# Eight experts on one core: weights as stationary 64-column blocks, and five of eight weight transfers behind a small transfer

## The chip, the cores and the metric

The kernel runs on one core of a Trainium2 chip. The metric is the device time of one execution in microseconds (us); less is better. Engines: PE (TensorE matmul), PEld (its weight load), DVE (VectorE), ACT (ScalarE), POOL (GpSimd), SP (SyncE, which issues transfers).

## What is computed

A recurrence (RWKV-7) over 768 steps for 4 x 8 heads gives 3072 rows x of 320 numbers. Each row goes to the one of eight experts with the largest gate; of an expert's rows the 80 with the largest gate weight are kept. Cut to what matters here, the rest is

```python
for e in range(E):                       # 8 experts
    tok_idx = ...                        # at most 80 rows
    h = np.maximum(x[tok_idx] @ w1[e], 0.0)                # 320 -> 1024
    out[tok_idx] = gate_w[tok_idx, None] * (h @ w2[e])     # 1024 -> 320
```

All numbers are float32; rows that are not kept stay zero in `out`.

## The kernel before

The kernel has three stages. In the first the recurrence is worked out in 24 units of 64 steps. Its instructions are recorded in a `Plan`, which puts them in an order by estimated times, and are then issued in that order. It ends with the ranking of gate weights (`rank_early` to `rank_last`, on DVE): `extract` (L842) takes the ten groups of eight largest values out of a row with MAX8 and MATCH_REPLACE8. The last two extracts work on `pair_a` and `pair_b` (L824), which are two buffers of `raww` in the pool `hold`. Gate and x rows of the last units go to DRAM (`x_rows`, L817).

Then the pool `hold` is closed, and a pool `wpool` takes its memory: all eight experts' weights get tiles of their own and are loaded by SP in turn (`load_expert`, L974 to L982; per expert `w1` as 128 x 2 x 1024, the remaining 64 rows of `w1` in two halves `w1r` on partitions 0 to 63 and 64 to 127, and `w2` as 128 x 8 x 320). Beside that, the second stage turns the ranking into lists of rows `idx_g` and `idx_s` (L1010 to L1051).

The third stage is the experts (from L1054 on). POOL gathers the 80 rows of each expert (`gather`). For expert e, `turn_x` turns the rows, `first_layer` holds x stationary (128 x 80) and moves the weights in 512 columns, ACT applies the ReLU, `turn_h` turns h in eight transposes with two DVE copies, `second_layer` holds h stationary and moves `w2` in 320 columns, DVE scales the result by the gate weight and POOL scatters it to `out`. The order in this stage is that of a scheduler, which starts from the order of the code:

```python
for e in range(E + 1):
    if e < E:
        first_layer(e)
    if e + 1 < E:
        turn_x(e + 1)
    if e > 0:
        second_layer(e - 1)
    if e < E:
        turn_h(e)
```

Of the kernel before, what the change touches and what calls it, by code (L numbers as in the profile page):

```python
# [145 lines left out]
def kernel(  # L146
# [77 lines left out]
    with ExitStack() as p1:  # L224
# [28 lines left out]
        def at(name, n):  # L253
            name, n = key_of(name, n)
            return buf[name][n % RINGS[name]]
# [7 lines left out]
        def bank(key):  # L263
            return plan.home[key]
# [556 lines left out]
            add(*args, sooner=LISTS[len(ranked)], **kw)  # L821

        ranked = []
        pair_a, pair_b = at("raww", NM), at("raww", NM + 1)  # L824

        def clear_tail(z):
            addr("POOL", 0.4, 0.1, z, lambda: nc.gpsimd.memset(la[:, capr:], 0.0), (), [("la", 0)])
# [1 line left out]
        def turn_gates(pieces, dst, key, z, bis):  # L829
            kc = ("gp", pieces[0][0])  # L830
            rows = pieces[0][1] * E

            def go():
                for j, (m0, nu) in enumerate(pieces):
                    nc.tensor.transpose(ps[0:rows, bank(kc), 128 * j : 128 * j + 128],
                                        gates[:, m0 : m0 + nu, :].rearrange("p m e -> p (m e)"), ident)
            addr("PE", 0.2 * len(pieces), 0.2, z, go, [("gates", b_) for b_ in bis], (), (kc, 1))
            addr("DVE", 0.25 + 0.001 * 128 * len(pieces), 0.1, z,
                lambda: nc.vector.tensor_copy(dst, ps[0:rows, bank(kc), 0 : 128 * len(pieces)]), [kc], [key])

        def extract(dst, src, z, src_key, dst_key):
            cols = src.shape[-1]  # L842
# [52 lines left out]
        def rank_late():  # L895
            ranked.append(1)
            z = 22 * PER
            turn_gates([(20, 1), (21, 1)], pair_a[0:E, 0:256], ("raww", NM), z, [5])
            clear_tail(z)
            extract(la[0:E], pair_a[0:E, 0:256], z, ("raww", NM), LA)  # L900
            merge(8, tops[0], tops[0], z, A0, A0)

        def rank_last():
            ranked.append(1)
            z = 24 * PER
            turn_gates([(22, 1), (23, 1)], pair_b[0:E, 0:256], ("raww", NM + 1), z, [6])
            extract(tops[1], pair_b[0:E, 0:256], z, ("raww", NM + 1), ("tops", 1))

        def late_adds():
            def late_consts():  # L910
# [70 lines left out]
        nc.sync.dma_start(w2, moe_w2[e].rearrange("(c p) d -> p c d", p=128))  # L981
        weights[e] = w1, w1r, w2  # L982

    for e in range(E):
        load_expert(e)

    idx_g = const.tile([cap, E], I32, name="idx_g")
# [71 lines left out]
    rows, xes, hs, hts = {}, {}, {}, {}  # L1059

    def gather(e):
        rows[e] = fs.tile([cap, XW], F32, name="rows", tag="rows", bufs=8)
        nc.gpsimd.indirect_dma_start(
            out=rows[e][:, 0:XW], out_offset=None, in_=x_dram[:, :],
            in_offset=bass.IndirectOffsetOnAxis(ap=idx_g[:, e : e + 1], axis=0))

    def turn_x(e):
# [8 lines left out]
        xes[e] = fs.tile([128, 3, cap], F32, name="xe", tag="xe")  # L1076
        nc.vector.tensor_copy(xes[e], xp)  # L1077

    def first_layer(e):
# [6 lines left out]
        for j in range(2):  # L1086
            half = slice(64 * j, 64 * j + 64)
            nc.tensor.matmul(hp[j], lhsT=xe[half, 2, :], rhs=w1r[half, :], start=False, stop=True)  # L1088
        hs[e] = fs.tile([cap, F], F32, name="h", tag="h")
        for j in range(2):  # L1090
            nc.scalar.activation(hs[e][:, FH * j : FH * j + FH], hp[j], Act.Relu)  # L1091

    def turn_h(e):
        h = hs.pop(e)
        hts[e] = fs.tile([128, FK, cap], F32, name="hT", tag="hT")
        for j in range(2):
            tp = ps_t.tile([128, FK // 2, cap], F32, name="tp", tag=f"t{j}")
            for f in range(FK // 2):
                o = FH * j + 128 * f
                nc.tensor.transpose(tp[:, f, :], h[:, o : o + 128], ident[:cap, :cap])  # L1100
            nc.vector.tensor_copy(hts[e][:, FK // 2 * j : FK // 2 * (j + 1), :], tp)  # L1101

    def second_layer(e):
        w2 = weights[e][2]
        hT = hts.pop(e)
        yp = ps_y.tile([cap, DM], F32, name="yp", tag="y")
        for f in range(FK):
            nc.tensor.matmul(yp, lhsT=hT[:, f, :], rhs=w2[:, f, :], start=f == 0, stop=f == FK - 1)  # L1108
        y = fs.tile([cap, DM], F32, name="y", tag="y")
        nc.vector.tensor_scalar_mul(y, yp, rows[e][:, DM : DM + 1])  # L1110
        nc.gpsimd.indirect_dma_start(  # L1111
            out=out[:, :], out_offset=bass.IndirectOffsetOnAxis(ap=idx_s[:, e : e + 1], axis=0),
            in_=y[:, :], element_offset=0, bounds_check=N - 1, oob_is_err=False, in_offset=None)

    for e in range(E):
        gather(e)
    turn_x(0)
    for e in range(E + 1):
        if e < E:
            first_layer(e)  # L1120
        if e + 1 < E:
            turn_x(e + 1)
        if e > 0:
            second_layer(e - 1)
        if e < E:
            turn_h(e)


# [24 lines left out]
```

## Time and profile before

| | |
|---|---|
| median of 3 runs (lowest, highest) | 560.91 us (559.71, 563.14) |
| the profiled execution, its own time | 561.64 us |
| its span | 559.6 us |
| PE busy | 425.6 us, 76% of the span |
| PEld busy | 331.6 us, 59% |
| DVE busy | 312.5 us, 56% |
| POOL busy | 224.1 us, 40% |
| ACT busy | 186.0 us, 33% |
| read and written in DRAM | 53.26 MB and 18.13 MB |

The span is what the profiler recorded of one execution; the time of that execution is 2.0 us longer. The shares are means over three stages with different limits, so a change to one stage is to be read from that stage's own rows. Times in the rows are us from the start of the span.

### The profile page before, as it was taken

To read this page: it belongs to the slowest core of one execution; us is meant where nothing else is said; L and a number is where in the kernel's file an instruction comes from. 1 tells how busy PE (TensorE), PEld (TensorE's weight loads), DVE (VectorE), ACT (ScalarE), POOL (GpSimd) and SP (SyncE) were. 2 spreads that over 40 slices of the span, in tenths; PEclk is the share of its full clock that TensorE was granted. 3 is DMA by queue.
4 is the path that set the end of the run, shared out by engine and by line. 5 is a ranking of instruction groups with operands and counts; after the bars stand their busy time and mean duration, and the time that the engine had idled before them with its cause. 6 is when DMAs were issued, how large, how long until landed. Compare 5 with 4: busy or idle time off the path is not lost. (4 is left out here: it accounts for less than half of the span.)

```text
span 559.6 us, 22079 instructions
## 1 busy us (share of the span) xinstructions
PE 425.6 (76%) x9617; PEld 331.6 (59%) x9617; DVE 312.5 (56%) x706; ACT 186.0 (33%) x361; POOL 224.1 (40%) x393
## 2 busy tenths in 40 slices
PE   2644089797928988889799998998895003999996
PEld 2543078686717877778687887887784002344443
DVE  4867977444703855684476644966678981121211
ACT  2432064353512453444443643445231000101010
POOL 7010011788388410898699516981000005010101
PEclk9978569798976999999899999999699555899999
DMA  8775367556593477676577374327200049999300
GB/s 133 113 116 112 64 154 133 99 94 133 96 243 81 99 174 134 149 132 117 133 143 172 100 132 116 75 44 161 71 16 27 23 143 342 326 332 344 104 15 16
DMA packets 241444, 72.91 MB, mean 130 GB/s; under 512 B 217908, under 2 KB 235716, under 8 KB 241348
## 3 DMA queue, kind: packets, MB, share of 16 engines
q1 hardware_dynamic: 211428, 65.50, 51.6%
q10 hardware_dynamic: 29152, 4.36, 4.9%
q0 software_dynamic: 768, 1.64, 1.0%
q8 instruction: 76, 1.25, 0.9%
q14 instruction: 20, 0.16, 0.1%
HBM read 53.26 MB, written 18.13 MB: 128 GB/s over the span
## 5 line engine op out<-in xcount | busy, mean ns | idle before, releaser
L498 POOL TENSOR_TENSOR tmp<-lt 128x30 f32<-128x30 f32 (+9 forms) x150 | 84.0, 560 | 61.0 <-DMA lt<-blocks 50.3
L500 POOL TENSOR_TENSOR lt<-lt,tmp 128x30 f32<-128x30 f32 (+9 forms) x150 | 88.8, 592 | 11.8
L707 DVE TENSOR_TENSOR UL<-ps,mask 128x832 f32<-128x832 f32 x24 | 24.5, 1022 | 54.0 <-PE ps L702 54.0
L758 PE MATMUL ps<-wsel,xT 128*128 128x192 f32 x192 | 40.7, 360 | 2.3 <-DVE xT L748 1.4
L1111 POOL DMA_INDIRECT out_dram<-y,idx_s x8 | 7.3, 917 | 74.6 <-DVE y L1110 74.6
L758 PEld LDWEIGHTS ps<-wsel,xT 128*128 128x128 f32 x192 | 34.2, 208 | 4.3 <-DVE xT L748 1.7
L369 DVE TENSOR_TENSOR_SCAN P<-dec,begins 128x520 f32<-128x520 f32 x24 | 31.4, 1313 | 9.4 <-ACT dec L365 9.3
L1108 PE MATMUL yp<-w,hT 128*80 128x320 f32 x128 | 35.9, 434 | 0.5 <-DVE hT L1101 0.5
L344 PE MATMUL ps<-ident,raww 128*128 128x128 f32 x88 | 16.6, 320 | 25.5 <-DMA raww<-in_w_dram 24.4
L344 PE MATMUL ps<-ident,kb 128*128 128x128 f32 x192 | 32.8, 297 | 3.6 <-DVE ends L373 1.8
L735 DVE TENSOR_TENSOR st<-ps,st 128x832 f32<-128x832 f32 (+1 forms) x24 | 23.8, 990 | 17.9 <-PE ps L724 17.9
L485 POOL MEMSET nt<- 32x1024 f32 x12 | 11.3, 945 | 54.6 <-ACT nt L417 54.2
L377 DVE TENSOR_TENSOR_SCAN iv<-dec,ends 128x520 f32<-128x520 f32 x24 | 30.2, 1259 | 4.0 <-ACT ivc L396 3.3
L1085 PE MATMUL hp<-w,xe 128*80 128x512 f32 x64 | 31.6, 641 | 0.5 <-DVE xe L1077 0.5
L452 DVE TENSOR_TENSOR psi<-ps,mask 128x512 f32<-128x512 f32 x24 | 16.4, 686 | 27.3 <-PE ps L437 23.0
L1091 ACT ACTIVATE h<-hp 80x512 f32<-80x512 f32 x16 | 8.6, 587 | 61.5 <-PE hp L1088 61.5
L611 ACT COPY rv<-ps 128x1024 f32<-128x1024 f32 x24 | 24.3, 1014 | 11.4 <-PE ps L344 6.5
L344 PEld LDWEIGHTS ps<-ident,raww 128*128 128x128 f32 x88 | 11.5, 162 | 27.4 <-DMA raww<-in_w_dram 15.1
L1108 PEld LDWEIGHTS yp<-w,hT 128*80 128x80 f32 x128 | 18.6, 150 | 14.7 <-issue 0.8
L344 PEld LDWEIGHTS ps<-ident,kb 128*128 128x128 f32 x192 | 22.8, 149 | 7.4 <-issue 3.7
L407 DVE TENSOR_TENSOR kb<-rawkb,ps 128x640 f32<-128x640 f32 x22 | 17.9, 813 | 15.5 <-PE ps L344 13.4
L1077 DVE COPY xe<-xp 128x240 f32<-128x240 f32 x8 | 3.3, 407 | 40.9 <-PE xp L1075 40.9
(171 smaller groups left out, 961.3 us busy)
## 6 DMA issues: line engine op xcount, KB each, us to landing
w<-in_moe_w_dram SPq DMA_DIRECT2D x8, 1280.0 KB
w<-in_moe_w_dram SPq DMA_DIRECT2D x8, 1024.0 KB, 16.4
VL<-in_v_dram SPq DMA_DIRECT2D x96, 40.0 KB, 2.3
out_dram<-zero SPq DMA_DIRECT2D x8, 480.0 KB, 4.2
raww<-in_w_dram SPq DMA_DIRECT2D x44, 80.0 KB, 2.8
rawkb<-in_k_dram SPq DMA_DIRECT2D x44, 80.0 KB, 3.6
rawkb<-in_b_dram SPq DMA_DIRECT2D x44, 80.0 KB, 3.2
rawr<-in_r_dram ACTq DMA_DIRECT2D x84, 40.0 KB, 2.9
```

Of the source, the lines that this page charges most:

```text
L344: nc.tensor.matmul(o, lhsT=i, rhs=ident, start=True, stop=True, is_transpose=True, skip_group_check=True)
L369: nc.vector.tensor_tensor_scan(at("P", n), at("dec", n)[:, 0 : H * SEG], begins, 0.0, op0=Alu.mult, op1=Alu.add)
L377: nc.vector.tensor_tensor_scan(at("iv", n)[:, H * SEG : 0 : -1], at("dec", n)[:, H * SEG : 0 : -1], at("ends", n)[:, H * SEG : 0 : -1], 0. ...
L407: nc.vector.tensor_tensor(out=view(at("kb", n), 0, (HB * H, 2), (HB, H), (1, D)), in0=view(at("rawkb", n), 0, (DM, 2), (D, H), (1, D)), in ...
L498: e.tensor_tensor(out=tv, in0=t3[:, 0:s, s : s + 1].to_broadcast([128, s, n]), in1=t3[:, s : s + 1, s + 1 :].to_broadcast([128, s, n]), op ...
L500: e.tensor_tensor(out=t3[:, 0:s, s + 1 :], in0=t3[:, 0:s, s + 1 :], in1=tv, op=Alu.add)
L611: nc.scalar.copy(at("rv", n).rearrange("p (k c) -> p k c", k=2), ps[:, bank(kr) : bank(kr) + 2, :])
L707: nc.vector.tensor_tensor(out=view(at("UL", n), 0, (M4 * X, 2), (1, M4 * X)), in0=view(ps[:, bank(ku), :], 0, (512, 2), (1, M4 * X)), in1= ...
L735: nc.vector.tensor_tensor(out=view(st, o, (BS, M4), (step, 2), (1, n_)), in0=view(flat, 512 * bank(ky) + o, (4 * T, M4), (step, 2), (1, n_ ...
L758: nc.tensor.matmul(ps[:, b0, WS * m : WS * m + WX], lhsT=at("xT", n)[:, 2 * T * cof(m, 0) : 2 * T * cof(m, 0) + 2 * T], rhs=wsel_[:, WS * ...
L1085: nc.tensor.matmul(hp[j], lhsT=xe[:, i, :], rhs=w1[:, i, FH * j : FH * j + FH], start=i == 0, stop=False)
L1108: nc.tensor.matmul(yp, lhsT=hT[:, f, :], rhs=w2[:, f, :], start=f == 0, stop=f == FK - 1)
```

## The change

1. `pair_a` and `pair_b` are now halves of the tile `begins`, which also lies in `hold`.
2. SP issues the weights of three experts where it issued all eight. Behind the first gather stands a transfer of one number out of the gathered rows to DRAM (`word`), and behind that the weights of the other five experts.
3. The first layer holds the weights stationary in blocks of 64 columns and moves x (80 columns); its output is h already turned, so `turn_h` goes. ACT applies the ReLU to one half, DVE to the other. The second layer holds blocks of 64 columns of `w2` stationary and moves h; its output is y turned. A new `turn_y` turns it back with two transposes and a matmul with `pair`, two 64 x 64 identities one above the other, which adds the two column halves of the last block; POOL makes `pair` with two copies.

```diff
-        pair_a, pair_b = at("raww", NM), at("raww", NM + 1)
+        pair_a, pair_b = begins[:, 0:256], begins[:, 256:512]
...
-    for e in range(E):
+    AHEAD = 3
+    for e in range(AHEAD):
         load_expert(e)
...
+    pair = fs.tile([128, HB], F32, name="pair", tag="pair", bufs=1)
+    nc.gpsimd.tensor_copy(pair[0:HB], ident[0:HB, 0:HB])
+    nc.gpsimd.tensor_copy(pair[HB:], ident[HB:, HB:])
...
     def first_layer(e):
-        hp = [ps_h.tile([cap, FH], F32, name="hp", tag=f"h{j}") for j in range(2)]
+        hp = [ps_h.tile([128, QF, cap], F32, name="hp", tag=f"h{j}") for j in range(2)]
         for i in range(2):
             for j in range(2):
-                nc.tensor.matmul(hp[j], lhsT=xe[:, i, :], rhs=w1[:, i, FH * j : FH * j + FH], start=i == 0, stop=False)
...
+                for b in range(NB):
+                    c = 64 * (b % 2)
+                    nc.tensor.matmul(hp[j][c : c + 64, b // 2, :], lhsT=w1[:, i, FH * j + 64 * b : FH * j + 64 * b + 64],
+                                     rhs=xe[:, i, :], start=i == 0 and b < 2, stop=False, skip_group_check=True)
+        for b in range(NB):
+            c = 64 * (b % 2)
+            for j in range(2):
+                half = slice(64 * j, 64 * j + 64)
+                nc.tensor.matmul(hp[j][c : c + 64, b // 2, :], lhsT=w1r[half, 64 * b : 64 * b + 64],
+                                 rhs=xe[half, 2, :], start=False, stop=True, skip_group_check=True)
         hts[e] = fs.tile([128, FK, cap], F32, name="hT", tag="hT")
...
+        nc.scalar.activation(hts[e][:, 0:QF, :], hp[0], Act.Relu)
+        nc.vector.tensor_scalar_max(hts[e][:, QF:, :], hp[1], 0.0)
...
     def second_layer(e):
-        yp = ps_y.tile([cap, DM], F32, name="yp", tag="y")
+        yp = ps_y.tile([128, 3, cap], F32, name="yp", tag="y", bufs=2)
         for f in range(FK):
-            nc.tensor.matmul(yp, lhsT=hT[:, f, :], rhs=w2[:, f, :], start=f == 0, stop=f == FK - 1)
+            for b in (0, 1, 2, 3, 4) if f % 2 == 0 else (1, 0, 3, 2, 4):
+                c = 64 * ((b + f) % 2) if b == 4 else 64 * (b % 2)
+                nc.tensor.matmul(yp[c : c + 64, b // 2, :], lhsT=w2[:, f, 64 * b : 64 * b + 64], rhs=hT[:, f, :],
+                                 start=f == 0 and b < 2, stop=f >= (FK - 2 if b == 4 else FK - 1), skip_group_check=True)
+        yts[e] = fs.tile([128, 3, cap], F32, name="yT", tag="yT")
+        nc.vector.tensor_copy(yts[e], yp)
+
+    def turn_y(e):
...
+        for i in range(2):
+            nc.tensor.transpose(yq[:, 128 * i : 128 * i + 128], yT[:, i, :], ident)
+        nc.tensor.matmul(yq[:, KW:], lhsT=yT[:, 2, :], rhs=pair, start=True, stop=True, skip_group_check=True)
...
+        nc.vector.tensor_scalar_mul(y, yq, rows[e][:, DM : DM + 1])
...
-    for e in range(E):
+    gather(0)
+    word = nc.dram_tensor("word", (1, 1), F32, kind="Internal")
+    nc.sync.dma_start(word[:, :], rows[0][0:1, 0:1])
+    for e in range(1, E):
         gather(e)
+    for e in range(AHEAD, E):
+        load_expert(e)
```

QF is 4 and NB is 8. Here is how the change moves instructions, at three places. In the lists, rows of equal instructions that follow each other are one with their count, and a bracket names the semaphores that an instruction waits for.

PE in the middle of the experts, before (w_3 is the `w1` or `w2` of the fourth expert, by the shapes; L1085 and L1088 are its first layer, L1108 the second, L1100 the turn of h, L1074 and L1075 the turn of x):

```order
L1108 MATMUL yp<-w_1_7004,hT 80x320 x8
L1100 MATMUL tp<-ident,h 128x80 x8
L1085 MATMUL hp<-w_3_7016,xe 80x512 x4
L1088 MATMUL hp<-w1r_7017,xe 80x512 x2
L1074 MATMUL xp<-ident,rows 128x80 x2
L1075 MATMUL xp<-ident,twice 128x80
L1108 MATMUL yp<-w_2_7011,hT 80x320 x8
```

PE in the middle of the experts, now (L1094 and L1100 are the first layer, L1113 the second, L1122 and L1123 the turn of y):

```order
L1113 MATMUL yp<-hT,w_3_7136 64x80 x5
L1122 MATMUL yq<-ident,yT 80x128 x2
L1123 MATMUL yq<-pair,yT 80x64
L1113 MATMUL yp<-hT,w_3_7136 64x80 x3
L1094 MATMUL hp<-xe,w_4_7141 64x80 x32
L1100 MATMUL hp<-xe,w1r_7142 64x80 x16
L1113 MATMUL yp<-hT,w_3_7136 64x80 x32
L1079 MATMUL xp<-ident,rows 128x80 x2
L1080 MATMUL xp<-ident,twice 128x80
L1113 MATMUL yp<-hT,w_4_7143 64x80 x5
```

The second layer of an expert now begins ahead of the next expert's first layer and is cut into pieces by the turns and by that layer.

SP at the weights, before (w_0 is the first expert's; L978 `w1`, L980 `w1r`, L981 `w2`):

```order
L978 DMA w_0_6995<-in_moe_w_dram 128x2x1024 [waits DMAHW2_49,DMAHW1_49,DMAHW3_49,DMAHW0_49,DMAHW4_49,DVE_49,DMAHW6_49,PE_49,DMAHW7_49,Activation_49,Pool_49]
L980 DMA w1r_6996<-in_moe_w_dram 64x512 x2
L981 DMA w_0_6997<-in_moe_w_dram 128x8x320
L978 DMA w_1_7002<-in_moe_w_dram 128x2x1024
L980 DMA w1r_7003<-in_moe_w_dram 64x512 x2
L981 DMA w_1_7004<-in_moe_w_dram 128x8x320
L978 DMA w_2_7009<-in_moe_w_dram 128x2x1024 [waits DMAHW1_49]
```

SP at the weights, now, from the first weight transfer to the fourth expert's:

```order
L979 DMA w_0_6995<-in_moe_w_dram 128x2x1024 [waits DMAHW2_49,DMAHW1_49,DMAHW3_49,DMAHW0_49,DMAHW4_49,DVE_49,DMAHW6_49,PE_49,DMAHW7_49,Activation_49,Pool_49]
L981 DMA w1r_6996<-in_moe_w_dram 64x512 x2
L982 DMA w_0_6997<-in_moe_w_dram 128x8x320
L979 DMA w_1_7002<-in_moe_w_dram 128x2x1024
L981 DMA w1r_7003<-in_moe_w_dram 64x512 x2
L982 DMA w_1_7004<-in_moe_w_dram 128x8x320
L979 DMA w_2_7009<-in_moe_w_dram 128x2x1024 [waits DMAHW1_49]
L981 DMA w1r_7010<-in_moe_w_dram 64x512 [waits DMAHW2_49]
L981 DMA w1r_7010<-in_moe_w_dram 64x512 [waits DMAHW3_49]
L982 DMA w_2_7011<-in_moe_w_dram 128x8x320 [waits DMAHW4_49]
L1132 DMA word<-rows 1x1 [waits DVE_49,DMASW0_49,PE_49,DMAHW5_49,Activation_49,Pool_49]
L979 DMA w_3_7134<-in_moe_w_dram 128x2x1024 [waits DMAHW6_49]
```

The first weight transfer names the same semaphores as before; the transfer to `word` stands between the third and the fourth expert and waits, among others, for the first gather (DMASW0). Twenty rows of weights are behind it.

POOL from the end of the first stage to the gathers, in the difference of the two orders (before, the first gather carried the waits that the first copy carries now):

```order
+L996 AFFINE_SELECT after_f<-ones 128x128 [waits DMAHW1_49,DMAHW2_49,DMAHW0_49,DMAHW3_49,DVE_49,DMAHW4_49,PE_49,DMAHW7_49,Activation_49,Pool_49]
+L1001 MEMSET seg 128x384
+L1005 IOTA iot_i 128x80
+L1002 MEMSET seg 128x8 [waits Pool_49]
+L1063 COPY pair<-ident 64x64 [waits PE_49,DVE_49,Activation_49,Pool_49]
+L1064 COPY pair<-ident 64x64
+L1068 DMA rows<-x_rows,idx_g 80x321 [waits Pool_49]
+L1068 DMA rows<-x_rows,idx_g 80x321 x7
```

Two copies now stand between the last index and the first gather.

## Rows read from the trace of the kernel before

**Rows 1.** Busy time by stretch, core 0: us, engines (instructions), granted clock, DMA share, GB/s

```profile
450.00:460.00 10.00, 1.04 (x3) 0.39 (x3) 8.16 (x22) 0.86 (x3) 0.89 (x4) 0.50 0.49 144
460.00:470.00 10.00, 2.13 (x24) 1.83 (x24) 3.29 (x9) 0.00 (x0) 3.85 (x4) 0.50 1.07 342
470.00:480.00 10.00, 7.56 (x13) 2.58 (x15) 0.41 (x1) 1.17 (x6) 3.62 (x4) 0.56 1.06 311
480.00:490.00 10.00, 9.68 (x42) 4.17 (x39) 1.79 (x4) 2.71 (x8) 0.00 (x0) 1.00 1.07 350
...
520.00:530.00 10.00, 10.00 (x41) 4.63 (x40) 1.75 (x4) 1.08 (x2) 0.91 (x1) 1.00 0.26 83
```

**Rows 2.** Timeline, PE and PEld in one expert: start us, busy us, engine, line

```profile
501.55 3.60 PE L1085 MATMUL hp<-w,xe 128*80 128x512 f32 x8
...
505.08 1.09 PE L1088 MATMUL hp<-w1r,xe 64*80 64x512 f32 x4
...
506.10 0.36 PE L1074 MATMUL xp<-ident,rows 80*128 80x80 f32 x2
...
506.36 4.47 PE L1108 MATMUL yp<-w,hT 128*80 128x320 f32 x16
...
510.40 0.83 PEld L1100 LDWEIGHTS tp<-ident,h 80*128 80x128 f32 x8
510.67 0.72 PE L1100 MATMUL tp<-ident,h 80*128 80x80 f32 x8
...
511.22 3.60 PE L1085 MATMUL hp<-w,xe 128*80 128x512 f32 x8
```

**Rows 3.** Groups by shape, PE: count, busy us, mean ns of one, idle before

```profile
L702 PE MATMUL ps<-W,nt 64*64 64x104 f32 x768 | 23.9, 263 | 1.0 <-DVE cd L839 0.8 <-POOL lt L500 0.2
...
L622 PE MATMUL ps<-rv 64*64 64x64 f32 x768 | 17.0, 226 | 1.6 <-issue 1.5
...
L1100 PE MATMUL tp<-ident,h 80*128 80x80 f32 x64 | 6.0, 234 | 0.3 <-ACT h L1091 0.3
```

**Rows 4.** Timeline, PE in the first stage: groups of four 64x64 tiles

```profile
405.50 0.94 PE L702 MATMUL ps<-W,nt 64*64 64x104 f32 x32
...
406.26 0.65 PE L622 MATMUL ps<-rv 64*64 64x64 f32 x32
```

**Rows 5.** Timeline at the start of the experts: SP's queue, DVE, POOL, PE

```profile
442.86 0.36 SPq L817 DMA_DIRECT2D x_rows<-xg  x1
...
453.46 0.42 DVE L846 MAX8 tops<-raww 8x8 f32<-8x256 f32 x1
...
454.08 0.37 SPq L978 DMA_DIRECT2D w<-in_moe_w_dram  x1
...
465.16 1.13 POOL L1063 DMA_INDIRECT rows<-x_rows,idx_g  x1 [10.09 <-DVE idx_s L1051]
...
473.24 6.43 PE L1085 MATMUL hp<-w,xe 128*80 128x512 f32 x8 [0.50 <-DVE xe L1077]
```

**Rows 6.** DMA issues: count, KB each, median us from issue to landing

```profile
w<-in_moe_w_dram SPq DMA_DIRECT2D x8, 1280.0 KB
w<-in_moe_w_dram SPq DMA_DIRECT2D x8, 1024.0 KB, 16.4
...
w1r<-in_moe_w_dram SPq DMA_DIRECT2D x16, 128.0 KB, 12.5
...
rows<-x_rows,idx_g POOLq DMA_INDIRECT x8, 6.7
out_dram<-y,idx_s POOLq DMA_INDIRECT x8, 2.5
```

**Rows 7.** Timeline at the end: the last y

```profile
554.95 0.55 DVE L1110 TENSOR_SCALAR y<-yp,rows 80x320 f32<-80x320 f32 x1 [4.23 <-PE yp L1108]
```

**Rows 8.** Groups by shape, POOL and DVE copies

```profile
L306 POOL COPY gt<-ident 32x256 f32<-32x256 f32 x2 | 0.8, 392 | 0.1
...
L1077 DVE COPY xe<-xp 128x240 f32<-128x240 f32 x8 | 3.3, 407 | 40.9 <-PE xp L1075 40.9
```

More of the change, by code (lines that the diff above doesn't have):

```diff
@@ L838, in turn_gates @@
             addr("DVE", 0.25 + 0.001 * 128 * len(pieces), 0.1, z,
-                lambda: nc.vector.tensor_copy(dst, ps[0:rows, bank(kc), 0 : 128 * len(pieces)]), [kc], [key])
+                lambda: nc.vector.tensor_copy(dst, ps[0:rows, bank(kc), 0 : 128 * len(pieces)]), [kc],
+                 [key] + [("begins", 0)] * (key[0] == "pair"))
         def extract(dst, src, z, src_key, dst_key):
@@ L897, in rank_late @@
             z = 22 * PER
-            turn_gates([(20, 1), (21, 1)], pair_a[0:E, 0:256], ("raww", NM), z, [5])
+            turn_gates([(20, 1), (21, 1)], pair_a[0:E, 0:256], ("pair", 0), z, [5])
             clear_tail(z)
-            extract(la[0:E], pair_a[0:E, 0:256], z, ("raww", NM), LA)
+            extract(la[0:E], pair_a[0:E, 0:256], z, ("pair", 0), LA)
             merge(8, tops[0], tops[0], z, A0, A0)
@@ L905, in rank_last @@
             z = 24 * PER
-            turn_gates([(22, 1), (23, 1)], pair_b[0:E, 0:256], ("raww", NM + 1), z, [6])
-            extract(tops[1], pair_b[0:E, 0:256], z, ("raww", NM + 1), ("tops", 1))
+            turn_gates([(22, 1), (23, 1)], pair_b[0:E, 0:256], ("pair", 1), z, [6])
+            extract(tops[1], pair_b[0:E, 0:256], z, ("pair", 1), ("tops", 1))
         def late_adds():
@@ L1058 @@
     ps_y = ctx.enter_context(tc.tile_pool(name="ps_y", bufs=1, space=PSUM))
-    rows, xes, hs, hts = {}, {}, {}, {}
+    rows, xes, hts, yts = {}, {}, {}, {}
+    pair = fs.tile([128, HB], F32, name="pair", tag="pair", bufs=1)
+    nc.gpsimd.tensor_copy(pair[0:HB], ident[0:HB, 0:HB])
+    nc.gpsimd.tensor_copy(pair[HB:], ident[HB:, HB:])
     def gather(e):
@@ L1077, in turn_x @@
         nc.vector.tensor_copy(xes[e], xp)
+    QF, NB = FK // 2, FH // 64
     def first_layer(e):
@@ L1081, in first_layer @@
         xe = xes.pop(e)
-        hp = [ps_h.tile([cap, FH], F32, name="hp", tag=f"h{j}") for j in range(2)]
+        hp = [ps_h.tile([128, QF, cap], F32, name="hp", tag=f"h{j}") for j in range(2)]
         for i in range(2):
             for j in range(2):
-                nc.tensor.matmul(hp[j], lhsT=xe[:, i, :], rhs=w1[:, i, FH * j : FH * j + FH], start=i == 0, stop=False)
[L1086 to L1094, printed above, removed]
-        hts[e] = fs.tile([128, FK, cap], F32, name="hT", tag="hT")
[L1096 to L1101, printed above, removed]
+                for b in range(NB):
[8 more added lines that the diff above has]
+                                 rhs=xe[half, 2, :], start=False, stop=True, skip_group_check=True)
+        hts[e] = fs.tile([128, FK, cap], F32, name="hT", tag="hT")
+        nc.scalar.activation(hts[e][:, 0:QF, :], hp[0], Act.Relu)
+        nc.vector.tensor_scalar_max(hts[e][:, QF:, :], hp[1], 0.0)
     def second_layer(e):
@@ L1105, in second_layer @@
         hT = hts.pop(e)
-        yp = ps_y.tile([cap, DM], F32, name="yp", tag="y")
+        yp = ps_y.tile([128, 3, cap], F32, name="yp", tag="y", bufs=2)
         for f in range(FK):
-            nc.tensor.matmul(yp, lhsT=hT[:, f, :], rhs=w2[:, f, :], start=f == 0, stop=f == FK - 1)
+            for b in (0, 1, 2, 3, 4) if f % 2 == 0 else (1, 0, 3, 2, 4):
[5 more added lines that the diff above has]
+    def turn_y(e):
+        yT = yts.pop(e)
+        yq = ps_t.tile([cap, DM], F32, name="yq", tag="yq")
+        for i in range(2):
+            nc.tensor.transpose(yq[:, 128 * i : 128 * i + 128], yT[:, i, :], ident)
+        nc.tensor.matmul(yq[:, KW:], lhsT=yT[:, 2, :], rhs=pair, start=True, stop=True, skip_group_check=True)
         y = fs.tile([cap, DM], F32, name="y", tag="y")
-        nc.vector.tensor_scalar_mul(y, yp, rows[e][:, DM : DM + 1])
+        nc.vector.tensor_scalar_mul(y, yq, rows[e][:, DM : DM + 1])
         nc.gpsimd.indirect_dma_start(
@@ L1122 @@
             turn_x(e + 1)
+        if e > 1:
+            turn_y(e - 2)
         if e > 0:
             second_layer(e - 1)
-        if e < E:
-            turn_h(e)
+    turn_y(E - 1)
 _INS = ["r", "k", "v", "w", "a", "b", "moe_w_gate", "moe_w1", "moe_w2"]
```

## The prediction

> **What bounds the kernel now.** I read the busy time by stretch first, then the PE timeline of one expert, then the start of the expert stage, then the DMA issues. [...] The DMA engines carry the weights from 454 us to about 522.5 us: 311 to 350 GB/s in the full stretches, and in 520 to 530 only 83 GB/s, that is 0.83 MB or some 2.5 us at the rate before. After that PE alone works, for another 32 us. So weights come early enough and the eight experts are bound by PE. The end hangs on PE too: the last y is scaled at 554.95 [rows 7], and from there to the end of the span (559.6) are 4.65 us that the change does not touch.
>
> One expert takes 9.68 us, from the first-layer group at 501.55 to the next at 511.22 [rows 2]: 3.53 us to the remainder (L1088), 1.02 to the turn of the next x, 0.26 to the second layer, 4.31 to the turn of h, and 0.55 for that. ACT, DVE and POOL have under 2 us each of work in it.
>
> **Part 1, the order of the weights.** The first weight transfer starts at 454.08, right behind the tenth MAX8 at 453.46 [rows 5]. In the changed order SP's first weight row still names the same semaphores, DVE among them, and in the built program the DVE count is in both kernels that of the last MAX8 into tops, which reads `begins` now and read `raww` before. Both tiles are in the pool that the weights replace. So I expect the weights at 454.1 again, no gain. What the last write of x_rows, issued at 442.86 [rows 5], would allow is the rival "does what it says".
>
> The small transfer stands on SP between the third and fourth expert and waits for the first gather, whose rows arrive about 6.7 us after issue [rows 6], at 471.9; twenty weight rows are queued behind it on SP. What hides that: one expert is 1024 + 1280 + 2 x 128 KB [rows 6], 2.62 MB, three are 7.86 MB, and the stretches moved 1.44 + 3.42 + 3.11 = 7.97 MB by 480 us [rows 1]. The transfers of the fourth expert are queued some 7 us before the first three run out. Cost 0. If that cover were gone, each us of gap would move the last weights past 522.5 by as much, which costs nothing either until PE catches up with them (below).
>
> On POOL two copies of 64x64 now stand between the last index and the first gather, and the gather waits for them. No such copy is in the trace; the nearest row is a copy of 32x256 in 0.39 us [rows 8], which bounds each from above, and nothing bounds them from below but 0.1 us. I take 0.5 us for both with the hand-over (ends 0.2 and 0.9). PE starts at 473.74 in place of 473.24 [rows 5].
>
> **Part 2, the experts.** A float32 matmul is two records in the trace (four matmuls of L1085 are x8). New per expert: 32 matmuls of the first layer (64 records), 16 of the remainder (32 records, half the rows), 40 of the second layer (80 records), all with 64 stationary and 80 moving columns. The turn of h goes (8 records), a turn of y comes (two transposes of 128 columns, one matmul of 64).
>
> What one record costs alone: eight transposes with 80 moving columns are 0.72 us, the last of them 0.234 long [rows 2, 3], so (0.72 - 0.234) / 7 = 0.070 us from start to start. The 512-column group agrees: 3.60 / 8 = 0.45 with the tail, 0.43 without, 0.84 ns a column, 0.067 for 80.
>
> What two records on the two column halves cost together is not in the trace: no group has 128 rows by 64 columns. The nearest is 64 rows by 64 columns, four tiles on two row halves and two column halves. There 32 records with 104 columns take 0.94 us and 32 with 64 columns 0.65 us [rows 4]. Take off the last record (0.263 and 0.226 [rows 3]) and share by seven steps of four records: 0.097 and 0.061 us a step, where one record of that length at 0.84 ns a column costs 0.087 and 0.054. So four records go in the time of 1.1 and the two column halves of the same rows do run beside each other. For pairs I take 0.070 us (ends: 0.067 and 0.078, that is 0.070 times 1.12; the far end, no overlap, is 0.140 and is a rival).
>
> Sum per expert: 32 + 8 + 40 = 80 steps of 0.070 are 5.60. Turn of x: 3 x 0.070 = 0.21. Turn of y: two of 128 columns at 0.11 and two records of 64 at 0.06, 0.34. Changes between tile shapes: 3.53 less 8 x 0.43 leaves 0.09, and 1.02 less 2 x 0.43 leaves 0.16 [rows 2]; the changed PE order has six of them per expert (the turns now stand inside the second layer), at 0.10 each 0.60. Together 6.75 us against 9.68, 2.93 less.
>
> **From start to end.** PE starts at 473.74 at the lower clock. Stretch 470 to 480 has a mean of 0.56 [rows 1], so the clock rose at about 478.8; I let it rise there again, since PE is as dense before it. The 5.1 us until then do 2.5 us of work; the first expert's first layer and remainder (40 steps and a change, 2.9) end at 479.2. To the end of the eighth expert's remainder are 7 x 6.75 = 47.25, less six steps of the second layer and one turn of y that stand behind it (0.42 + 0.44), plus two waits for a copy out of PSUM (0.8): 526.4. Then six steps (0.5), the wait for yT (a record's 0.23, a DVE copy of 0.41 [rows 8] and hand-over, 0.75), a turn of y (0.5), 40 steps (2.8), yT again (0.75) and the last turn (0.7): y is scaled at 532.4 instead of 554.95. With 22.5 us off, the span is 559.6 - 22.5 = 537.1, and the profiled run of 561.64 becomes 539.1. That run is 0.7 us above the median of 560.91, so the median may be a little lower; I say 539.
>
> What is late next: the eighth first layer begins at about 526.4 - 2.9 = 523.5, and the last weights are there at 522.5. With a cheaper step PE would wait for weights, so a gain of much over 23 us is not to be had. At 0.067 the sum would be 1.9 us lower and meets that limit at 537. At 0.078 it is 80 x 8 x 0.008 = 5.1 us higher, 544.
>
> [...] Eight loads of 128 columns (0.83 us from 510.40) and eight transposes on the same 80 rows (0.72 us from 510.67) [rows 2] are both over by 511.4, a stretch of 1.0; in turn they would need 1.55. [...]
>
> **The rivals.**
> 1. *The steps are dearer in a long run.* PE now issues 176 loads and 176 matmuls in 80 steps per expert, one expert after another; a cost that comes only with such length would not show in a group of 32. The busy time of L1100 with its tail gives 0.72 / 8 = 0.090 a step: 0.020 x 640 = 12.8 us, 552. Against it: the sets of four above issue more records per us than this needs.
> 2. *The change does what it says*: weights from 443.3. The three experts would be in by 467, the gathers would land in 2.5 us, as the scatters do [rows 6], instead of 6.7, and PE would start 4 us earlier: 535. Against it: the unchanged wait for DVE.
> 3. *The column halves take turns*, because both need all 128 rows, which no tile in the trace does. Then each of the 72 pairs costs 0.140: 72 x 0.070 x 8 = 40.3 us more, 579, slower than before. It decides above the point where 22.5 / (72 x 8) = 0.039 is added to a pair, that is at 0.109 us a pair. Against it: four tiles, two on each row half, ran at 1.1 times one.
>
> **Chances.** My forecast 0.66, rival 1 0.17, rival 2 0.05, rival 3 0.09, something between that ends near the old time 0.03. Two runs of this kernel can be told apart at about 1%. Faster by over 1%: 0.66 + 0.17 + 0.05 = 0.88; within 1%: 0.03; slower: 0.09. The range goes from 533 (rival 2 with the cheap step) to 553 (rival 1) and leaves out rival 3.
>
> **What would show it.** Right: first weight issue near 454.1, the first gather near 465.6, PE's first-layer groups of 64 records in about 2.3 us, an expert in 6.8 us, y of the last expert near 532. A group of 64 records in 4.5 us is rival 3; in 2.9 us rival 1. If PE idles for weights before the seventh or eighth expert, part 1 was not free. If weights start at 443, the wait was misread.

## The result, and the profile after

The changed kernel takes 556.37 us (median of 20 runs, 548.88 to 564.61), the kernel before 560.86 us (20 runs, 555.05 to 570.76). The ratio is 0.9897, 95% interval 0.9869 to 0.9925: about 1% faster. Some executions of either kernel are one to three per cent slower than the others; the ratios here and below leave these out, so they are not the ratios of the medians. The forecast was 539.0 us with a range up to 553; the gain by the ratio is about a quarter of the one forecast.

The two profiled executions differ by 5.05 us (561.64 and 556.59), their spans by 4.9 (559.6 and 554.7). To read that, I cut the span at four points that stand in the timeline: the last write of x_rows, the first layer's start on PE, the last scaled y, the end.

| | last x_rows | PE starts | last y | end | PE start to last y |
|---|---|---|---|---|---|
| before [rows 5, 7] | 442.86 | 473.24 | 554.95 | 559.6 | 81.7 |
| forecast | 442.86 | 473.74 | 532.4 | 537.1 | 58.7 |
| after | 444.71 | 475.07 | 548.68 | 554.7 | 73.6 |

The first stage, whose work is the same, ended 1.85 us later in this execution. From the last x_rows to PE's start both take 30.4 us. The experts take 8.1 us less, where 23 had been forecast, and the end 1.4 us more. So the question is what the experts did with 15 us.

**The start** (timeline of after; start us, us, engine, line), which answers to [rows 5] and [rows 8]:

```profile
444.71 0.36 SPq L817 DMA_DIRECT2D x_rows<-xg  x1
...
455.31 0.42 DVE L847 MAX8 tops<-begins 8x8 f32<-8x256 f32 x1
...
455.92 0.38 SPq L979 DMA_DIRECT2D w<-in_moe_w_dram  x1
...
466.23 0.23 POOL L1063 COPY pair<-ident 64x64 f32<-64x64 f32 x1 [9.31 <-DVE idx_s L1053]
466.50 0.23 POOL L1064 COPY pair<-ident 64x64 f32<-64x64 f32 x1
467.09 1.13 POOL L1068 DMA_INDIRECT rows<-x_rows,idx_g  x1 [0.36 <-POOL pair L1064]
...
473.79 0.96 SPq L1132 DMA_DIRECT2D word<-rows  x1
...
475.07 4.53 PE L1094 MATMUL hp<-xe,w 128*64 128x80 f32 x64 [0.50 <-issue]
```

The first weights still start right behind the last MAX8 (455.92; MAX8 at 455.31). They do not begin at the last x, which was written 11 us earlier. The two copies into `pair` take 0.23 us each, and PE starts 19.15 us after the first weights, against 19.16 before: what they cost was hidden.

**An expert late in the stage** (timeline of after, PE and the first layer's weight loads; in the brackets the idle time and what ended it), which answers to [rows 2]:

```profile
532.41 2.29 PEld L1094 LDWEIGHTS hp<-xe,w 128*64 128x64 f32 x64
...
532.48 2.39 PE L1094 MATMUL hp<-xe,w 128*64 128x80 f32 x64
534.80 0.78 PE L1100 MATMUL hp<-xe,w1r 64*64 64x80 f32 x32
...
537.06 0.42 PE L1122 MATMUL yq<-ident,yT 128*80 128x128 f32 x2 [0.50 <-DVE yT L1116]
...
539.94 2.40 PE L1094 MATMUL hp<-xe,w 128*64 128x80 f32 x64
```

64 records take 2.39 us. The forecast named about 2.3 as its own mark, 2.9 as rival 1's and 4.5 as rival 3's, so the price of a step held: (2.39 - 0.23) / 31 steps is 0.070 us. From one first layer to the next are 7.46 us, with a wait of 0.50 for yT.

**The middle of the stage** looks different. Stretches of after (us; busy time and instructions of PE, PEld, DVE, ACT, POOL; granted clock, DMA share, GB/s), which answer to [rows 1]:

```profile
480.00:490.00 10.00, 8.29 (x232) 7.60 (x224) 2.02 (x5) 1.50 (x6) 0.00 (x0) 0.98 1.06 328
490.00:500.00 10.00, 9.05 (x188) 8.38 (x189) 2.02 (x5) 1.10 (x5) 0.95 (x1) 0.83 1.07 344
...
510.00:520.00 10.00, 5.87 (x145) 5.44 (x146) 0.49 (x1) 0.44 (x1) 0.92 (x1) 0.89 1.07 319
...
530.00:540.00 10.00, 9.50 (x254) 8.93 (x251) 2.25 (x5) 0.44 (x1) 1.82 (x2) 1.00 0.06 17
...
488.30:490.85 2.55, 0.24 (x8) 0.08 (x5) 0.00 (x0) 0.00 (x0) 0.00 (x0) 0.95 1.07 343
490.85:495.00 4.15, 4.15 (x78) 3.89 (x79) 0.13 (x1) 0.18 (x1) 0.00 (x0) 0.62 1.06 368
...
515.70:518.85 3.15, 0.23 (x7) 0.07 (x3) 0.00 (x0) 0.00 (x0) 0.00 (x0) 0.85 1.06 391
518.85:524.80 5.95, 5.95 (x67) 5.30 (x69) 1.36 (x3) 0.00 (x0) 0.91 (x1) 0.51 1.07 280
```

In before, PE was busy 9.68 to 10.00 of 10 at clock 1.00 here. Now it is busy 5.87 of 10 in one stretch, and has whole gaps (the fifth and seventh row) in which no other engine works either and only the DMA engines run. Behind the two longest gaps the granted clock is 0.62 and 0.51 on average over 4 and 6 us, so it is at its lower level (0.50, as from 460 to 470 us in [rows 1]) for most of that time. When the weights are in (530 to 540, 17 GB/s) the picture is the forecast's again: clock 1.00, and only the wait for yT.

The timeline names what ended the gaps (after, PE):

```profile
490.79 3.19 PE L1094 MATMUL hp<-xe,w 128*64 128x80 f32 x42 [2.31 <-issue]
...
503.90 0.49 PE L1100 MATMUL hp<-xe,w1r 64*64 64x80 f32 x12 [1.50 <-issue]
...
511.21 2.01 PE L1094 MATMUL hp<-xe,w 128*64 128x80 f32 x50 [1.34 <-issue]
...
513.87 2.00 PE L1113 MATMUL yp<-hT,w 128*64 128x80 f32 x46
518.80 1.60 PE L1113 MATMUL yp<-hT,w 128*64 128x80 f32 x18 [2.92 <-issue]
```

"issue" is time in which the engine waited for nothing that the profile shows: no semaphore that it has, so by the profile neither a transfer nor another engine. The last pair of rows says more. The gap stands in the middle of one expert's second layer: 46 of its records had just run, with the same h and the same weight tile that the following ones read. From the start of the last record ahead of a gap to the first behind it the four gaps are 2.5, 1.7, 1.6 and 3.2 us, 9.0 in all.

What is it that PE lacked? The queues of the DMA view have one of kind "instruction". In after it moved 85 packets and 1.39 MB in the whole span, 16 KB each. Here is that queue's row from 481 to 526 us, while the weights come (after; packets, MB, share of 16 engines):

```profile
q8 instruction: 7, 0.11, 1.1%
```

In before the same 45 us needed 2 packets, for 182 records of PE and 182 of PEld (before):

```profile
q8 instruction: 2, 0.03, 0.3%
```

```profile
481.00:526.00 45.00, 44.68 (x182) 20.37 (x182) 8.47 (x20) 6.88 (x21) 3.71 (x4) 1.00 0.98 310
```

Over the whole span after has nine packets more than before (85 and 76), and 2304 records of PE and PEld more (21538 and 19234), which is 9 x 256. So this queue brings PE's own program; the DMA view counts its packets on the same 16 engines as those of the weights (1.1% beside 101.8%, 481 to 526 in after). The changed kernel needs some four times as much of it here (1625 records against 364). How much is a packet? The stretches of after, the same 45 us and those that hold what ran between one gap and the next, count it:

```profile
481.00:526.00 45.00, 36.56 (x812) 33.44 (x813) 7.94 (x19) 3.61 (x15) 3.71 (x4) 0.89 1.06 322
...
490.00:503.40 13.40, 11.44 (x254) 10.52 (x254) 2.02 (x5) 1.10 (x5) 0.95 (x1) 0.87 1.06 343
503.40:510.80 7.40, 5.97 (x127) 5.31 (x127) 2.26 (x5) 0.83 (x3) 0.94 (x1) 1.00 1.07 324
510.80:518.00 7.20, 4.66 (x128) 4.24 (x128) 0.49 (x1) 0.44 (x1) 0.92 (x1) 0.99 1.09 301
```

The 45 us have 1625 records of PE and PEld to 7 packets, 232 each. Between the gaps lie 508, 254 and 256: the gaps stand 512, 256 and 256 records apart, if a few missing ones are allowed for. Counted from the program's start, with the records of PE's sequencer, the gaps of after follow record 19393, 19905, 20161 and 20417, those of part 2 alone (below) 19137, 19393, 19905 and 20417: always a multiple of 256 apart. Neither tiles nor weights have that period, for an expert has some 360 records. By the trace's own times the packets start 6.3 to 8.0 us apart until the weights end, and 3.6 to 5.4 behind that; each of the four gaps ends 1.26 to 1.32 us after a packet has landed. The same times show when a packet comes, if blocks of 256 records are counted from the gaps: it starts only once PE is in the block ahead of the one that it brings. Behind the weights' stream that is 0.1 to 0.9 us after PE entered that block, under it 3.3 to 5.6 us. That is theory F (fetch): under the weights' stream a packet of 256 instructions comes more slowly (6.3 to 8.0 us apart) than PE uses it up. Two rivals stood against it: W, the experts wait for late weights, and T, PE itself hangs between the small tiles, whatever the DMA engines do.

**The end** (timeline of after), which answers to [rows 7]:

```profile
548.68 0.55 DVE L1125 TENSOR_SCALAR y<-yq,rows 80x320 f32<-80x320 f32 x1 [0.64 <-PE yq L1123]
550.56 0.91 POOL L1126 DMA_INDIRECT out_dram<-y,idx_s  x1 [4.11 <-issue]
```

The last scatter starts 1.33 us after y is done (549.23). In before it was 0.27 us.

### The profile page after: what moved, and what is told of

Its sections match the earlier page's. It is cut to its first block, busy times and chain, and to the rows that moved or that the text cites. A ratio compares the mean times of both kernels' runs of the same rounds, so it can differ in the third digit from the quotient of the medians.

```text
span 554.7 us, 24382 instructions
## 1 busy us (share of the span) xinstructions
PE 408.7 (74%) x10769; PEld 354.3 (64%) x10769; DVE 311.2 (56%) x706; ACT 181.4 (33%) x353; POOL 223.5 (40%) x395
## 3 DMA queue, kind: packets, MB, share of 16 engines
q8 instruction: 85, 1.39, 1.0%
## 5 line engine op out<-in xcount | busy, mean ns | idle before, releaser
L758 PEld LDWEIGHTS ps<-wsel,xT 128*128 128x128 f32 x192 | 32.9, 202 | 4.3 <-DVE xT L748 1.7
L1113 PE MATMUL yp<-hT,w 128*64 128x80 f32 x640 | 29.4, 245 | 3.3 <-issue 3.1
L1113 PEld LDWEIGHTS yp<-hT,w 128*64 128x64 f32 x640 | 26.0, 144 | 5.3 <-issue 3.6
L1094 PE MATMUL hp<-xe,w 128*64 128x80 f32 x512 | 23.9, 256 | 4.1 <-issue 4.1
L1104 DVE TENSOR_SCALAR hT<-hp 128x320 f32<-128x320 f32 x8 | 3.9, 492 | 39.9 <-PE hp L1100 39.9
L702 PE MATMUL ps<-W,nt 64*64 64x104 f32 x768 | 25.2, 267 | 1.3 <-ACT gt L568 0.6
```

The costliest lines, as they stand in the source:

```text
L702: nc.tensor.matmul(ps[T * bb : T * bb + T, b0 + q, X * i : X * i + X], lhsT=tm[rows, q, i, :], rhs=at("W", n)[rows, wo : wo + X], start=Tr ...
L758: nc.tensor.matmul(ps[:, b0, WS * m : WS * m + WX], lhsT=at("xT", n)[:, 2 * T * cof(m, 0) : 2 * T * cof(m, 0) + 2 * T], rhs=wsel_[:, WS * ...
L1094: nc.tensor.matmul(hp[j][c : c + 64, b // 2, :], lhsT=w1[:, i, FH * j + 64 * b : FH * j + 64 * b + 64], rhs=xe[:, i, :], start=i == 0 and ...
L1113: nc.tensor.matmul(yp[c : c + 64, b // 2, :], lhsT=w2[:, f, 64 * b : 64 * b + 64], rhs=hT[:, f, :], start=f == 0 and b < 2, stop=f >= (FK ...
```

## The experiments

All ratios are to the kernel before, with 95% intervals.

**Part 1 alone, part 2 alone.** The first has `pair_a` and `pair_b` in `begins`, three experts' loads, `word` and the five loads behind it, with the experts of before. The second has the changed experts, and `pair_a`, `pair_b` and the weights as in before, that is, against the changed kernel:

```diff
-    AHEAD = 3
+    AHEAD = E
...
-    nc.sync.dma_start(word[:, :], rows[0][0:1, 0:1])
```

> Part 1 of the change alone (the halves of begins, three experts' weights first, five behind the small transfer), with the experts of before. The first weights still wait for the last MAX8, and PE is the bound of this stage, so every theory expects no change: first weight issue within 0.3 us of the end of the last MAX8, 9.7 us per expert, ratio 1.00 (0.995 to 1.005). If the order of the weights had cost the changed kernel its gain, this would be some 1 to 2% slower than before.

> Part 2 alone (the experts with 64-column blocks), with the weights in the order of before and no small transfer. Fetch theory (PE's own instructions come in 16 KB packets over the DMA engines that carry the weights, each some 7 us after the one before while the weights stream, and PE uses one up in under 5 us): the stalls put down to issue stay, about 8 to 9 us in all before 526 us, ratio near that of the whole change, 0.99 (0.985 to 0.995). If the small transfer or the later issue of five experts' weights made the stalls, they go, and the ratio is 0.97.

*Measured.* Part 1 alone: 561.02 us, ratio 0.9989 (0.9948 to 1.0031), no difference. Part 2 alone: 557.37 us, 0.989 (0.9807 to 0.9973), the whole of the change. Its gaps are the same, at other places (timeline, PE):

```profile
493.10 2.87 PE L1093 MATMUL hp<-xe,w 128*64 128x80 f32 x42 [2.66 <-issue]
...
506.26 0.35 PE L1099 MATMUL hp<-xe,w1r 64*64 64x80 f32 x3 [2.04 <-issue]
...
520.67 1.52 PE L1112 MATMUL yp<-hT,w 128*64 128x80 f32 x19 [2.30 <-issue]
```

So neither the order of the weights nor the small transfer makes the gaps. The gaps stand in all three parts of an expert: first layer, remainder, second layer.

**No later loads.** The last five experts take the weights of the first three, and their own loads are left out; the experts' matmuls are as many as in the changed kernel:

```diff
 for e in range(AHEAD, E):
-    load_expert(e)
+    weights[e] = weights[e % AHEAD]
```

> The changed kernel without the weight loads of the last five experts, which use the tiles of the first three instead: it leaves out 13.1 MB of transfers, the instructions of PE are the same. Fetch theory: once the three experts' weights are in (about 480 us) no stall put down to issue is left but for one at the start, instruction packets come as PE asks for them, an expert takes 7.0 to 7.5 us all along, and the time is 13 us lower than that of the changed kernel, 543 (540 to 546). Late-weights theory (PE waits for weights whose wait the profile does not show): the same, so this run does not part the two. Tile theory (64-column tiles or changes of tile shape hang PE up, whatever the DMA engines do): the stalls of 1.5 to 3 us stay, 556.

539.04 us, 0.9578 (0.9502 to 0.9654), a little under the 540 to 546 expected. Stretches, the instruction queue from 481 to 526, and one expert in the timeline:

```profile
481.00:526.00 45.00, 44.28 (x1197) 42.17 (x1195) 10.36 (x25) 4.52 (x17) 4.63 (x5) 0.96 0.24 64
...
490.00:500.00 10.00, 10.00 (x282) 9.68 (x281) 2.76 (x7) 1.32 (x6) 0.95 (x1) 1.00 0.05 14
```

```profile
q8 instruction: 10, 0.16, 1.6%
```

```profile
512.12 2.38 PE L1094 MATMUL hp<-xe,w 128*64 128x80 f32 x64
...
518.67 2.38 PE L1094 MATMUL hp<-xe,w 128*64 128x80 f32 x64
```

With the DMA engines free, PE is busy 10.00 of 10 from 490 to 500 and in the three stretches of 10 us behind it, ten packets come in the 45 us in which seven came, and no gap is left behind 489 (one of 0.76 us at 488, while the three experts' weights were still on the way, follows record 19137). 282 and 281 records in 10 us use up 256 in 4.5 us, less than the 6.3 to 8.0 us of after. An expert takes 6.55 us (forecast 6.75; 7.0 to 7.5 expected of this run), and from PE's start to the last y are 57.0 us (479.36 to 536.36; forecast 58.7). T falls: the same tiles run without a gap. F and W are both left, since both live on the stream, though W has no reason for the 256.

**The second layer of before.** The weights and the new first layer stay; the second layer again holds h and moves 320 columns, 16 records in place of 80:

```diff
+    WIDE_UP_TO = 8
...
+    def second_layer_wide(e):
...
+            nc.tensor.matmul(yp, lhsT=hT[:, f, :], rhs=w2[:, f, :], start=f == 0, stop=f == FK - 1)
...
-            second_layer(e - 1)
-    turn_y(E - 1)
+            (second_layer_wide if e - 1 < WIDE_UP_TO else second_layer)(e - 1)
```

> The changed kernel with the second layer of the kernel before (h stationary, 128x80, weights moving in 320 columns; no turn of y). Weights, their order and the first layer stay as changed. An expert then has some 230 PE instructions in place of about 380 and needs about 7.7 us, so 256 instructions last some 8.5 us, longer than the 6.3 to 7.9 us in which packets of instructions followed each other under the weights stream. Instruction theory: the issue stalls of PE go or shrink to under 2 us in all, its clock stays at 1.00 from the second expert on, and 8 x 7.7 = 61.6 us from 475.1 with 2.5 us for the slow start and 0.6 for the last y end at about 540: the span is some 545, ratio 0.97, faster than the changed kernel although an expert alone is a us dearer. Rival (weights come late): an expert is only 1 us longer, so of the 9 us of stalls about 4 stay, with their drop of the clock: ratio about 0.985.

544.71 us, 0.972 (0.9635 to 0.9804). An expert is dearer by 1.2 us than the changed one without gaps (7.75 from 501.79 to 509.54, against 6.55), and the kernel is 1.8% faster. The instruction queue and the stretch, and one expert:

```profile
q8 instruction: 6, 0.10, 1.0%
```

```profile
481.00:526.00 45.00, 45.00 (x668) 31.25 (x666) 8.12 (x18) 3.79 (x14) 4.67 (x6) 1.00 0.97 304
```

```profile
501.79 2.43 PE L1095 MATMUL hp<-xe,w 128*64 128x80 f32 x64
...
509.54 2.43 PE L1095 MATMUL hp<-xe,w 128*64 128x80 f32 x64
```

The weights come at the same rate (the share of the DMA engines is 1.05 to 1.07 from 490 to 520) and start as far behind the last x_rows, 11.2 us. PE is busy all 45 us, and the clock stays at 1.00. 668 and 666 records in 45 us use up 256 in 8.6 us, longer than the 6.3 to 8.0 us from one packet to the next in after. W gave 0.985, which lies outside the interval.

**Early weights, and both edits together.** The buffers of the first stage that come free early got a pool of their own, and the first three experts' weights take its memory, so that they wait only for the last turned x and no longer for the last MAX8:

```diff
+        hold_a = p1.enter_context(tc.tile_pool(name="hold_a", bufs=1))
...
+        FIRST_FREE = ("dec", "raww", "rawa", "rawkb", "rawr", "P", "ah", "kb")
...
-    wpool = ctx.enter_context(tc.tile_pool(name="wpool", bufs=1))
+    wfirst = ctx.enter_context(tc.tile_pool(name="wfirst", bufs=1))
...
+    wlast = ctx.enter_context(tc.tile_pool(name="wlast", bufs=1))
```

> The changed kernel, with the pool of the first stage cut in two, so that the tiles under the first three experts' weights are free when the last turned x is read, and with the first weight row ahead of the last write of x_rows. The weights should start near 430 in place of 456 and the last be there near 501; the gathers then have a freer queue and PE starts 3 to 4 us sooner. Instruction theory: PE still starves while weights are on the way, that is up to about 501 (two or three stalls, 3 to 5 us in all), and not behind it: ratio 0.96 to 0.975. Rival (weights come late): each expert's weights are there 20 us before it begins, so there is no stall at all, and the ratio is 0.945 to 0.955.

> Both edits at once: early weights and the second layer of the kernel before for all experts. Instruction theory: no stalls (256 instructions last longer than a packet needs), but all eight experts cost 7.7 us: PE starts 3 to 4 us sooner than in the run with late weights, ratio about 0.965. Rival (weights come late): no stalls either, and slower than early weights alone by 8 x 0.7 = 6 us.

549.63 us, 0.9782 (0.9699 to 0.9866), and 547.63 us, 0.9749 (0.9665 to 0.9832). With early weights alone the first weight row starts at 435.55, 13.6 us ahead of the last x_rows (449.17), and PE starts 27.1 us behind that write instead of 30.4. The weights are 20 us earlier, and the gaps are still there (timeline, PE):

```profile
435.55 0.38 SPq L981 DMA_DIRECT2D w<-in_moe_w_dram  x1
...
496.30 1.68 PE L1097 MATMUL hp<-xe,w 128*64 128x80 f32 x42 [2.05 <-issue]
...
503.68 1.33 PE L1116 MATMUL yp<-hT,w 128*64 128x80 f32 x33 [2.48 <-issue]
...
510.91 0.35 PE L1103 MATMUL hp<-xe,w1r 64*64 64x80 f32 x2 [2.91 <-issue]
```

That decides against W, which expected no gap and 0.945 to 0.955. F expected 3 to 5 us of gaps and 0.96 to 0.975; it got 7.4 us by the brackets (2.05 + 2.48 + 2.91; 8.1 measured as the 9.0 of after were), a stall in the first expert besides (below), and a ratio a little above. The size was missed in part because the stream did not end at 501, but near 511 (stretches of early weights alone):

```profile
500.00:510.00 10.00, 5.53 (x162) 5.11 (x158) 0.51 (x2) 0.44 (x1) 0.95 (x1) 1.00 1.07 330
510.00:520.00 10.00, 9.09 (x192) 8.75 (x192) 2.06 (x5) 0.84 (x4) 0.94 (x1) 0.83 0.20 66
```

Behind 511 there is no such gap. With the old second layer as well there is none from the second expert on, but the ratio is no better than with late weights and above the 0.965 expected; the earlier start was given back (below).

**A mix.** Old second layer for the experts that run under the stream, the changed one for the others: four and four with early weights, five and three with late ones.

```diff
+    WIDE_UP_TO = 4
...
-            second_layer(e - 1)
...
+            (second_layer_wide if e - 1 < WIDE_UP_TO else second_layer)(e - 1)
```

> Early weights, the second layer of the kernel before for the first four experts and the changed one for the last four. Instruction theory: no stalls under the weights stream, and the short expert (7.0 us in place of 7.7) behind it: some 3 us below early weights with the old second layer throughout, ratio about 0.96, the fastest of these. Rival (weights come late): slower by some 3 us than early weights with the changed second layer throughout.

> Weights in the changed order and at the changed time; the second layer of the kernel before for the first five experts, the changed one for the last three. It tells what the early weights add to the mix. Instruction theory: the stream ends near 523, five experts of 7.7 us end at about 513 and the sixth may meet one stall of up to 2.5 us under it; the span is 3 x 0.7 = 2 us under the run with the old second layer throughout, less that stall: ratio 0.966 to 0.972. If early weights carry the gain of the early mix (0.9606), this stays at 0.972; if the mix alone carries it, this comes to about 0.963.

The first comparison gave 540.71 us, 0.9606 (0.9498 to 0.9714) for the early mix and 545.31 us, 0.9747 (0.9663 to 0.9831) for the late one. That would have been worth 1.4% to the early weights, but in the two traces the first stage had ended 5 us apart. So both ran again, side by side:

> The early mix once more, beside the late mix on one chip. In their first traces the two take the same time from the last write of x_rows to the last scaled y (92.7 and 93.1 us); the first stage ended 5 us apart. If early weights are worth nothing beyond that, the two ratios agree within 0.8% here; if the first ratios (0.961 and 0.975) were the kernels' own, they stay 1.4% apart.

> The late mix beside the early mix: about 0.968 for both if early weights are worth nothing, 0.975 if they carry what the first comparison showed. Both stay below the changed kernel (0.990).

543.79 us, 0.9728 (0.9662 to 0.9794), and 544.84 us, 0.974 (0.9659 to 0.9821): too close to be told apart, so no gain of the early weights is shown here. Both lie above what had been expected at first (about 0.96 for the early mix, 0.966 to 0.972 for the late one). Either mix beats both kernels (the changed one: 0.9869 to 0.9925); from the old second layer throughout (0.972) they cannot be told apart. By the traces, from PE's start to the last y the late mix takes 62.4 and 63.2 us and the old second layer throughout 64.8; that gain of 2 us was expected, and is below what the times tell.

Why does the early start give nothing? In the early mix, PE's first expert (timeline, PE) begins 27.1 us after the last x_rows, and then stalls:

```profile
472.31 3.46 PE L1098 MATMUL hp<-xe,w 128*64 128x80 f32 x47 [0.50 <-DVE xe L1085]
476.10 0.54 PE L1098 MATMUL hp<-xe,w 128*64 128x80 f32 x3 [0.33 <-issue]
477.54 0.51 PE L1098 MATMUL hp<-xe,w 128*64 128x80 f32 x3 [0.90 <-issue]
```

Until 479 the records come singly or in threes, "issue" again, and the clock is 0.50 from 470 to 480 and 0.78 from 480 to 490. So it takes 65.8 us from PE's start to the last y, 3.4 more than the first run of the late mix. The stall begins behind record 18882, within two of a multiple of 256 ahead of the gaps of early weights alone (19393, 19649, 19905), so where PE enters a new block. But the block itself had come with the packet that landed at 430.9, if packets are counted back from those gaps, and the records do not stop but come slowly. Here the stall ends when the next packet lands, at 478.9; in early weights alone the same stall, behind record 18883, ends at 483.0, ahead of the landing at 483.9. So F as it stands does not explain this stall, and what PE waits for in it stays open.

**Blocks of 128 columns.** If the number of instructions is the matter, half as many wider blocks should do the same work:

```diff
-                for b in range(NB):
...
+                for f in range(QF):
+                    o = FH * j + 128 * f
+                    nc.tensor.matmul(hp[j][:, f, :], lhsT=w1[:, i, o : o + 128], rhs=xe[:, i, :],
```

> The changed kernel with stationary blocks of 128 columns in place of pairs of 64 (the last 64 columns of the second layer stay in pairs): as many steps of 80 columns per expert (80), the same weights at the same time, but 103 records per expert in place of 183. Fetch theory: an expert uses 206 loads and matmuls in 6.8 us, 256 in 8.4, which is more than the 7 us between packets, so the stalls go or shrink under 1 us each, and the time is 540 to 545, ratio 0.965 to 0.973. Late-weights theory: the weights land as late as before, so the stalls stay and it is 556. Tile theory: it goes down too, since nearly all 64-column tiles are gone; the run without later loads tells that from the fetch.

629.62 us, 1.1206 (1.1143 to 1.1269): a clear miss. One stretch, and one first layer with its weight loads (timeline, PEld and PE):

```profile
600.00:610.00 10.00, 10.00 (x58) 9.69 (x58) 0.41 (x1) 0.00 (x0) 0.00 (x0) 0.50 0.00 0
```

```profile
549.48 7.00 PEld L1094 LDWEIGHTS hp<-xe,w 128*128 128x128 f32 x32
...
549.67 7.04 PE L1094 MATMUL hp<-xe,w 128*128 128x80 f32 x32
```

There are no gaps, but the clock is at 0.50 to the end, with PE busy 10.00 of 10. And a record takes 7.00 / 32 = 0.22 us, as long as its weight load; at the higher clock half of that, 0.11, is an estimate from this row. I had expected the 0.070 of a record of 80 columns. [rows 2] would have told: eight loads of 128 columns are 0.83 us there, 0.104 each. Loads of 64 columns come at 2.29 / 64 = 0.036 us each (PEld of the first layer at 532.41 in after), so two of them take 0.072, about the step of 0.070, and one of 128 took 0.104. By the estimate of 0.11 an expert of 103 such records would cost about 11 us even at the higher clock, more than the 9.68 of before.

## Why the prediction was wrong, by its own steps

- *Part 1 costs and gains nothing, weights behind the last MAX8.* Right, by the rows of the start and by part 1 alone (0.9989). Rival 2, weights at the last x, did not come true. The run with early weights made it true, and PE then started 3.3 us sooner (4 in the rival); its ratio of 0.9782 still has the gaps in it, and with the mix no gain of the earlier start is left to see.
- *Copies into `pair`: 0.5 us.* They take 0.23 each, but PE's start did not move against the first weights.
- *A step of 0.070, two column halves beside each other.* Right: 0.070 in after, and an expert of 6.55 us with the stream taken away (forecast 6.75). Rival 3 would have shown 4.5 us for 64 records. In after the 64 loads take 2.29 us and the 64 matmuls on the same 128 rows 2.39, side by side.
- *The sum from start to end, 8 x 6.75.* This is the step that failed. I had counted the 176 loads and 176 matmuls of an expert, and gave them no price of their own beside that of their execution. What they need besides is a supply of instructions (seven packets of 16 KB from 481 to 526 in after), and the sum had no term for it; after showed 9.0 us of gaps for it, and the lower clock (0.62 and 0.51) behind two of them. Against rival 1, "a cost that comes only with such length", I argued that sets of four in the first stage issue more records per us. They do; a stretch of before shows what I had not looked at beside it:

```profile
300.00:400.00 100.00, 93.61 (x2909) 81.72 (x2898) 62.83 (x152) 45.02 (x85) 51.95 (x91) 0.95 0.51 115
```

256 records in 4.4 us, as dense as the experts, but with 115 GB/s on the DMA engines and not 320. The rival had the right kind of cause and, with 552 us, nearly the right size, which is luck, as it comes from 0.020 us on each of 640 steps; its mark, a dearer step, did not come, since the cost stands between the groups.
- *The size.* From PE's start to the last y 73.6 us were measured and 58.7 forecast, 14.9 more. The four gaps are 9.0. The lower clock behind two of them costs, by an estimate from their stretches, 4.15 x (1 - 0.62) + 5.95 x (1 - 0.51) = 4.5. Together 13.5; the remaining 1.4 I can't put down to a row.
- *The clock rises once and stays.* It rose some 5 us after PE's start, as forecast (after: 0.50 from 470 to 480, 0.98 from 480 to 490, so near 480.4), and fell again behind the gaps of 2.5 and 3.2 us, not behind those of 1.6 and 1.7. The length alone does not decide it: in early weights alone the clock stayed at 1.00 (490 to 510) behind gaps of 2.3 and 2.7 us and fell behind one of 3.1 (0.83 from 510 to 520).
- *The end, 4.65 us that the change does not touch.* 6.0 in after. The row of the last scatter names no releaser, and why it starts 1.3 us late stays open. The other runs shown have 5.0 (early mix) and 5.3 us (no later loads).
- *"A gain of much over 23 us is not to be had", for want of weights.* Not reached.

F is shown from both sides: take the stream away and the same instructions run without a gap (PE busy 30.00 of 30 us from 490 to 520); keep the stream and take instructions away, and there is none either (45.00 of 45 from 481 to 526); move the weights, and the gaps end with the stream (near 511 in early weights alone). In after a packet's own transfer takes 1.1 to 1.25 us under the stream; what grows there is the time before its start (3.3 to 5.6 us), and what it waits for in that time is not shown.

## What to carry to other kernels

PE's instructions were traffic here too, 16 KB for 256 records. So count the records per us of a new inner loop, and compare the time in which it uses up such a packet with the distance of packets of the instruction queue while the DMA engines are full. Under the stream 8.6 us for a packet ran without a gap, and the instructions that use one up in 4.5 us without the stream did not. So few wide instructions fitted under this weight stream, and many small ones only behind it. And gaps that the timeline puts down to "issue", with every other engine idle and the DMA engines full, were the sign of it (1.6 to 3.2 us each in after, at a DMA share of 1.05 to 1.07); behind the two longest the price of a lower clock came on top, 4.5 us by the estimate above.

## What the runs showed of the hardware that was not expected

- Instruction packets of PE start 6.3 to 8.0 us apart beside a weight stream of 322 GB/s, and ten came in 45 us without it, as fast as PE used them up (2392 records, 9.3 times 256).
- With 128-column stationary blocks the granted clock stayed at 0.50 although PE was busy 10.00 of 10 and PEld 9.69. With 64-column blocks and as much PE busy time it was 1.00 (no later loads). Why is open.
- A weight load of 128 columns took 0.104 us at clock 1.00 [rows 2] and 0.22 at 0.50. Loads of 64 columns on alternating column halves came at 0.036 us each at 1.00 (0.07 at 0.50: 16 in 1.10 us in the run with wide blocks), so two of them took less time than one of 128.
